# A convolution and an attention in one kernel: the block factors move to the copy of the seeds, and the first unit's maxima are taken 1024 pairs at a time

## The chip, the core and the metric

The kernel runs on one core of a Trainium2 chip. The metric is the time of the whole program on the device in microseconds (us). A core has a matrix engine (PE, with its weight loads shown as PEld), a vector engine (DVE), a scalar engine (ACT), a general engine (POOL) and a queue that issues transfers (SP). Each takes its instructions in program order and waits for the others by semaphores. Matrix results land in PSUM, eight banks of 128 x 512 float32; everything else lies in SBUF.

## What is computed

Two results are put side by side, each 2048 x 448. One is a long convolution of `u` with a kernel `K` made from complex powers, the other a full attention with 16 heads of 28 channels.

```python
# A: u [2048, 448]
P = exp((A * dt)[:, :, None] * pos)          # A complex, [448, 256]
K = 2.0 * einsum("dn,dnl->dl", C, P).real    # [448, 2048]
a = irfft(rfft(u_t, 4096) * rfft(K, 4096))[:, :2048].T + u * D_skip
# B: x [2048, 448]
q, k, v = split_heads(x @ wqkv)              # 16 heads of 28
p = softmax(q @ k.T * 28 ** -0.5)
b = concat_heads(p @ v) @ wo
return concatenate([a, b], -1)
```

## The kernel before

**First stage** (lines 213 to 536). The projections of `x` are made and written to DRAM as high and low halves, and seeds of the powers are made for each of the 56 blocks of 8 channels and written to DRAM too (`sd_d`). Four pools hold PSUM there: `ps_w` (three buffers `pm`), `ps_t` (two buffers `pt`), `ps_n`, `ps_x` (lines 219 to 222). At its end (lines 528 to 535) the maxima of the first unit are taken. A unit is 512 queries of a group of 4 heads; there are 16. The softmax subtracts a query's maximum over all 2048 keys, which is put as two rows into the query tile `qhat`, so that the score product already holds it. For each head and each 128 queries (`i`, 16 of them) `max_mm` makes four products: `kc` 0 is the query times the difference of two key halves (`kdif`), of which ACT takes the positive part (`rl`); `kc` 1 is the query times the second half, and DVE adds `rl` and takes the maximum, so that one operation covers 512 pairs of keys; `kc` 2 and 3 are plain products over 512 keys each, which DVE reduces. `max_join` takes the maximum of the three partial results, `max_end` turns it and `max_put` writes it into `qhat` by two transfers. `more` (line 528) deals the products out to the five buffers `pt` and `pm`. A scheduler may move instructions in this first stage.

**The loop** (lines 1007 to 1070) has 256 steps, 16 for each unit, and from line 856 on every instruction stays in program order. Each step walks through `ORDER` (line 34): `m0 s0 m1 s1 v f pv f v k m2 s2 m3 s3 w v`. `s` is a score product of 128 keys and its exponential on ACT, `pv` the products of the previous step with the values. `m0` to `m3` are the four products of `max_mm` for the unit after next. `f` is a slot for one background task, taken from queues (`slot`, line 950): the three products of a block of the convolution kernel (`m_due`: `part0` twice and `part1`), the transform of `u` (`u_due`), output projections (`p_due`), and, late in the loop, `spectrum` tasks and then `finish` tasks (`f_slot`). `v` takes one operation from the queue `powers["g"]` for DVE. `k` may begin a block and issues up to three operations from `powers["e"]` for POOL.

**A block** of the convolution kernel: `load_sd` brings its seeds `sdb`; `k_seeds` (line 605) copies the seeds of `e` at its first call and those of `g` at its second, one call at `k` of a step; `k_factors` (line 615) makes `fz` from three parts of `sdb` by three DVE operations of 128 x 96, both operands of each in SBUF; `k_start` (line 622) copies a part of `fz` to PSUM (`zg`) on ACT; `e_power` (line 626) issues nine POOL operations that build `e` from its seeds and `fz`; `g_powers` (line 640) gives nine DVE operations that build `g`, each with one operand in PSUM. `k_begin` (line 976) starts block `b` when `K0 + b * KP <= s` (`KP` is 3.5 steps) **and** both queues `powers` are empty. It fills them: nine operations of `g_powers`, then `k_factors` of the next block as a tenth entry (lines 982 and 983), and nine of `e_power`. The block's products fall due 4, 5 and 6 steps later (`KD`, line 990).

**Hand-over** (line 1015): when no block is left, the PSUM banks of `ps_g` and `ps_m` become one pool of four (`ps_f`), which the second half of the `spectrum` tasks needs. `spectrum` (line 768) multiplies with `u`'s transform on DVE (`pr`) and combines on POOL (`p`, 64 x 448, four a job); `finish` (line 811) loads `ut`, scales it on POOL and adds it on DVE (`ot`). A `finish` job is loaded three steps ahead (`FL`). What is left after the last step runs in the loop at line 1074.

Of the kernel before, what the change touches and what calls it, by code (L numbers as in the profile page):

```python
# [8 lines left out]
F32 = mybir.dt.float32  # L9
F32R = mybir.dt.float32r  # L10
I32 = mybir.dt.int32
AF = mybir.ActivationFunctionType
ALU = mybir.AluOpType
AX = mybir.AxisListType
PSUM = bass.MemoryType.PSUM
# [8 lines left out]
HG = H // G  # L24
CQ = 512
NQ = L // CQ
# [24 lines left out]
NB = D // 8  # L51
# [40 lines left out]
def body(ctx, tc, a, out):  # L92
    nc = Engines(tc)
# [4 lines left out]
    def pool(stack, name, bufs=1, space=None, side=None):  # L98
        kw = {} if space is None else {"space": space}
        if side:  # L100
            kw["side"] = side
        return stack.enter_context(tc.tile_pool(name=name, bufs=bufs, reuse_waits="tile", **kw))
# [21 lines left out]
    ps_w, n_ring = [None, 3], [0]  # L124
# [6 lines left out]
    q_p = pool(att, "q_p", side="right")  # L131
# [12 lines left out]
    kt_g, kd_g, q_u, m_u, mh_u, o_u, rl_u = {}, {}, {}, {}, {}, {}, {}  # L144
# [29 lines left out]
    def max_mm(u, i, kc, ps=w_tile):  # L174

        if i == 0 and kc == 0:
            m_u[u] = q_p.tile([128, HG, 4, 3], F32, name="mx", bufs=2)
        j, t = divmod(i, 4)
        pm = ps()
        q, kt = q_u[u][:, j, t * 128:(t + 1) * 128], kt_g[u // NQ][j]  # L180
        mx = m_u[u][:, j, t, max(kc - 1, 0):max(kc - 1, 0) + 1]
        if kc == 0:
            nc.tensor.matmul(pm, q, kd_g[u // NQ, j], start=True, stop=True)
            rl_u[u, i] = kd_p.tile([128, CQ], F32, name="rl", bufs=2)
            nc.scalar.activation(rl_u[u, i], pm, AF.Relu)
        elif kc == 1:
            kb = kt.rearrange("p (c s n) -> p c s n", c=NQ, s=2)[:, :2, 1, :]
            nc.tensor.matmul(pm.rearrange("p (c n) -> p c n", c=2), q, kb, start=True, stop=True)
            rl = rl_u.pop((u, i))
            nc.vector.tensor_tensor_reduce(rl, pm, rl, 1.0, -3.0e38, ALU.add, ALU.max, mx)  # L190
        else:
            nc.tensor.matmul(pm, q, kt[:, kc * CQ:(kc + 1) * CQ], start=True, stop=True)
            nc.vector.tensor_reduce(mx, pm, axis=AX.X, op=ALU.max)

    def max_join(u):
        m_u[u, 1] = q_p.tile([128, HG * 4], F32, name="m1", bufs=2)
        nc.vector.tensor_reduce(m_u[u, 1], m_u[u].rearrange("p a b c -> p (a b) c"), axis=AX.X, op=ALU.max)

    def max_end(u, ps):
        nc.tensor.transpose(ps[:16, :128], m_u[u, 1], ident)  # L200
        mh = q_p.tile([16, 2, 128], F32R, name="mh")
        nc.vector.tensor_scalar(mh[:, 0, :], ps[:16, :128], -1.0, None, op0=ALU.mult)
        nc.vector.scalar_tensor_tensor(mh[:, 1, :], ps[:16, :128], -1.0, mh[:, 0, :].bitcast(F32),
                                       op0=ALU.mult, op1=ALU.subtract)
        mh_u[u] = mh

    def max_put(u):
        for i in range(2):
            nc.sync.dma_start(q_u[u][DH + i:DH + i + 1, :, :].rearrange("p h (t q) -> p (h t) q", t=4).bitcast(F32),
                                mh_u[u][:, i, :].bitcast(F32))  # L210


    with ExitStack() as st:
        sst, xst, wst = ExitStack(), ExitStack(), ExitStack()
        t_p = pool(sst, "t_p")
        s_p = pool(sst, "s_p")
        x_p = pool(xst, "x_p")
        y_p = pool(wst, "y_p", side="right")
        ps_w[0] = pool(st, "ps_w", 1, PSUM)
        ps_t = pool(st, "ps_t", 2, PSUM)  # L220
        ps_n = pool(st, "ps_n", 2, PSUM)
        ps_x = pool(st, "ps_x", 1, PSUM)

        xns = {}

# [35 lines left out]
        t = a["A_log_dt"]  # L261
# [263 lines left out]
                for c in range(NQ):  # L525
                    load_v(0, c)
        xst.close()
        more = [lambda: ps_t.tile([128, CQ], F32, name="pt")] * 2 + [w_tile] * 3
        for i in range(16):
            for kc in range(4):  # L530
                max_mm(0, i, kc, more[(4 * i + kc) % 5])
        nc.scalar.activation(half_pi[:1], half_pi[:1], AF.Exp)
        max_join(0)
        max_end(0, ps_t.tile([128, CQ], F32, name="pt"))
        max_put(0)
        sst.close()


# [66 lines left out]
    def k_seeds(b):  # L605

        if b not in es:
            es[b] = e = g_p.tile([128, 2, 16, N2], F32, name="e", bufs=2)
            nc.scalar.activation(e[:, :, :, :8], sds[b][:, :F_G].rearrange("p (c h e) -> p c h e", c=2, e=8), AF.Copy)
        else:  # L610
            g = g_p.tile([128, 2, 16, N1], F32, name="g", bufs=2)
            nc.scalar.activation(g[:, :, :, :4], sds[b][:, F_G:F_Z].rearrange("p (c h e) -> p c h e", c=2, e=4), AF.Copy)
            egs[b] = es.pop(b), g

    def k_factors(b):
        fzs[b] = fz = g_p.tile([128, 3, 6 * 16], F32, name="fz", bufs=2)
        mg, cs, sn = (sds[b][:, F_Z + 96 * i:F_Z + 96 * i + 96] for i in range(3))
        nc.vector.tensor_tensor(fz[:, 0], mg, cs, ALU.mult)
        nc.vector.tensor_tensor(fz[:, 2], mg, sn, ALU.mult)
        nc.vector.scalar_tensor_tensor(fz[:, 1], mg, -1.0, sn, op0=ALU.mult, op1=ALU.mult)  # L620

    def k_start(b):
        zgs[b] = ps_g.tile([128, CQ], F32, name="zg")
        nc.scalar.activation(zgs[b][:, :Z_G].rearrange("p (f n) -> p f n", f=3), fzs[b][:, :, 48:], AF.Copy)

    def e_power(b, i, q):

        t, m = egs[b][0], 8 << i
        zz = fzs[b].rearrange("p f (k h) -> p k f h", k=6)
        if q == 0:  # L630
            zr = zz[:, i, 0, :][:, None, :, None].to_broadcast([128, 2, 16, m])
            nc.gpsimd.tensor_tensor(t[:, :, :, m:2 * m], t[:, :, :, :m], zr, ALU.mult)
        elif q == 1:
            uts[0] = g_p.tile([128, 2, 16, 32], F32, name="eu")[:, :, :, :m]
            zi = zz[:, i, 1:3, :][:, :, :, None].to_broadcast([128, 2, 16, m])
            nc.gpsimd.tensor_tensor(uts[0], t[:, ::-1, :, :m], zi, ALU.mult)
        else:
            nc.gpsimd.tensor_tensor(t[:, :, :, m:2 * m], t[:, :, :, m:2 * m], uts[0], ALU.add)

    def g_powers(b):  # L640

        t, zg = egs[b][1], zgs[b]
        zz = zg[:, :Z_G].rearrange("p (f k h) -> p k f h", k=3, f=3)
        tt = nc.vector.tensor_tensor

        def first(i, m):
            tt(t[:, :, :, m:2 * m], t[:, :, :, :m], zz[:, i, 0, :][:, None, :, None].to_broadcast([128, 2, 16, m]), ALU.mult)

        def second(i, m, c):
            n = c.stop - c.start  # L650
            u = zg[:, CQ // 2:CQ // 2 + n * 16 * m].rearrange("p (c h m) -> p c h m", c=n, m=m)
            zi = zz[:, i, 1 + c.start:1 + c.stop, :][:, :, :, None].to_broadcast([128, n, 16, m])
            tt(u, t[:, ::-1, :, :m][:, c], zi, ALU.mult)
            return lambda: tt(t[:, c, :, m:2 * m], t[:, c, :, m:2 * m], u, ALU.add)
        both, u = slice(0, 2), {}

        def lowest():
            first(0, 4)
            second(0, 4, both)()
        ops = [lowest, lambda: first(1, 8), lambda: u.update(a=second(1, 8, both)), lambda: u["a"](), lambda: first(2, 16)]  # L660
        for c in (slice(0, 1), slice(1, 2)):
            ops += [lambda c=c: u.update(a=second(2, 16, c)), lambda: u["a"]()]
        return ops
# [196 lines left out]
        max_mm(1, 0, kc)  # L860
    for _ in range(2):
        k_seeds(0)
    k_factors(0)

    urgent, back = collections.deque(), collections.deque()
    powers = {"g": collections.deque(), "e": collections.deque()}
# [109 lines left out]
    def k_begin(s_):  # L976
        if not (k_due and K0 + k_due[0] * KP <= s_ and k_due[0] in egs and not powers["e"] and not powers["g"]):
            return
        b = k_due.popleft()
        k_start(b)  # L980
        powers["g"] += g_powers(b)
        if b + 1 < NB:
            powers["g"].append(lambda: k_factors(b + 1))
        powers["e"] += [lambda i=i, q=q: e_power(b, i, q) for i in range(3) for q in range(3)]
        p0, p1, p2 = k_mm(b)

        def m1():
            p1()
            done["mm"] = b
        m_due.extend((s_ + KD + i, t_) for i, t_ in enumerate((p0, m1, p2)))  # L990
        last[0] = b
# [15 lines left out]
    for s in range(NS):  # L1007
        u, kt = divmod(s, NK)
        sm = s + NK + min(LEAD, 1 + s // 2)
        more = s in (2, 4)  # L1010
# [62 lines left out]
    s = NS  # L1073
# [65 lines left out]
```

## Time and profile before

| what | value |
|---|---|
| median of three runs | 1309.37 us (1307.53 to 1311.9) |
| the profiled execution | 1310.93 us |
| its span in the profile | 1308.8 us |
| granted PE clock, mean | 0.98 |
| the last two score products start | from 1274.75 us of the span on |

The profile gives times from the start of the span. A row of a timeline has the start, the time taken, the engine, and output<-input by the program's names; "x2" merges two neighbours, and a bracket gives the idle time before and what ended it. A row of a group has busy time and the mean of one in ns. Every program line that issues an instruction goes through one helper, so all rows bear its line L76, and one goes by names. The rows that the argument needs stand in the prediction.

### The profile page before, as it was taken

The page shows a single profiled execution, that of the slowest core. Times are in us where ns is not written, and L with a number is a line of the kernel's source. Part 1 is how long each engine was busy: PE and PEld are TensorE (multiplying, and loading weights), DVE is VectorE, ACT ScalarE, POOL GpSimd, SP SyncE. Part 2 cuts the span into 40 slices and gives each one's busy share as a digit, 9 for nine tenths or more (in the row PEclk, how much of TensorE's full clock was granted, in tenths as well). Part 3 has the DMA queues.
Part 4 walks back from the last instruction along what each step waited for, and adds up shares of the span by engine and source line. Part 5 has one row for each costly group of instructions (what it writes and reads, how often), then busy time and mean ns, then how long its engine had stood idle before and what let it go on. Part 6 is the DMA issues. An engine that isn't in the chain of part 4 may idle for free.

```text
span 1308.8 us, 32327 instructions
## 1 busy us (share of the span) xinstructions
PE 1225.8 (94%) x12177; PEld 686.0 (52%) x12177; DVE 948.6 (72%) x2194; ACT 963.7 (74%) x2048; POOL 839.0 (64%) x656
## 2 busy tenths in 40 slices
PE   6888976899999999999999999999999999999996
PEld 5666853455555555555555555555555555454332
DVE  5676678878877887777788888888888958453221
ACT  4878873588888888888878888888877657565451
POOL 2455641467777787777788888878879849235341
PEclk9989988899999999999999999999999999999998
DMA  6777779546864545487524225431454533269577
GB/s 195 230 255 267 260 235 294 157 93 153 183 151 105 126 147 167 112 215 196 155 71 95 74 51 136 109 96 39 109 151 124 171 99 107 82 187 287 170 228 192
DMA packets 200084, 205.30 MB, mean 157 GB/s; under 512 B 95992, under 2 KB 158520, under 8 KB 197880
## 3 DMA queue, kind: packets, MB, share of 16 engines
q1 hardware_dynamic: 199928, 203.24, 55.3%
q8 instruction: 96, 1.57, 0.5%
q14 instruction: 60, 0.49, 0.1%
HBM read 120.74 MB, written 82.18 MB: 155 GB/s over the span
## 4 chain that ended last, share of the span: by engine, by line
PE 71%; DVE 8%; DMA 4%; POOL 4%; ACT 3%; issue 2%; SPq 1%; POOLq 0%; DVEq 0%; ACTq 0%
PE pm L76 40%; PE pss L76 16%; PE po L76 16%; DVE mx L76 2%; DMA ut<-in_A_u 2%; POOL p L76 1%; DVE rl L76 1%; ACT tri L76 1%; DVE tri L76 1%; POOL e L76 1%; SPq L76 1%; DVE pr L76 1%; DVE mh L76 1%; ACT sg L76 1%; DVE fz L76 1%
## 5 line engine op out<-in xcount | busy, mean ns | idle before, releaser
L76 ACT ACTIVATE p<-pss 128x512 f32<-128x512 f32 x1024 | 561.9, 610 | 127.9 <-PE pss L76 125.7
L76 DVE TENSOR_REDUCE mx<-pm 128x1 f32<-128x512 f32 x500 | 321.7, 684 | 128.7 <-PE pm L76 127.6
L76 PE MATMUL pss<-qhat,khat 128*128 128x512 f32 x1024 | 403.0, 400 | 0.7 <-ACT p L76 0.6
L76 PE MATMUL pm<-khat,qhat 128*128 128x512 f32 x749 | 330.3, 443 | 9.6 <-DVE mx L76 6.8
L76 POOL TENSOR_TENSOR e<-e,fz 128x256 f32<-128x256 f32 x168 | 203.2, 1209 | 202.3 <-PE pss L76 84.0
L76 PE MATMUL po<-p,v 128*32 128x512 f32 x2048 | 269.8, 594 | 0.0
L76 PEld LDWEIGHTS pm<-khat,qhat 128*128 128x128 f32 x749 | 141.5, 189 | 220.1 <-DVE mx L76 41.5
L76 POOL TENSOR_TENSOR e<-e,eu 128x256 f32<-128x256 f32 x168 | 247.9, 1475 | 13.2
L76 PEld LDWEIGHTS pss<-qhat,khat 128*128 128x128 f32 x1024 | 190.5, 189 | 40.3 <-issue 9.6
L76 POOL TENSOR_TENSOR eu<-e,fz 128x256 f32<-128x256 f32 x168 | 201.7, 1200 | 0.0
L76 DVE CUSTOM_DVE_ANT_0 rl<-pm,rl 128x512 f32<-128x512 f32 x249 | 170.8, 686 | 31.6 <-ACT rl L76 27.3
L76 ACT ACTIVATE rl<-pm 128x512 f32<-128x512 f32 x249 | 151.0, 606 | 19.3 <-PE pm L76 18.9
L76 DVE TENSOR_TENSOR g<-g,zg 128x128 f32<-128x128 f32 x392 | 162.1, 413 | 3.6
L76 POOL TENSOR_TENSOR p<-pr,pr 64x448 f32<-64x448 f32 x64 | 73.3, 1146 | 96.9 <-PE pm L76 61.7
L76 PE MATMUL pm<-xh,khat 112*128 112x512 f32 x256 | 89.0, 430 | 20.6 <-DVE kb L76 7.8
L76 PE MATMUL pm<-kdif,qhat 128*128 128x512 f32 x249 | 102.2, 410 | 4.4 <-DVE pr L76 2.2
L76 DVE TENSOR_TENSOR zg<-g,zg 128x128 f32<-128x128 f32 x224 | 87.7, 392 | 4.7
L76 PEld LDWEIGHTS pm<-e,g 128*32 128x32 f32 x3584 | 58.2, 109 | 45.6 <-issue 23.5
L76 DVE TENSOR_TENSOR pr<-pm,ub 128x448 f32<-128x448 f32 x64 | 36.9, 619 | 53.5 <-PE pm L76 38.7
L76 ACT ACTIVATE y<-pm 128x448 f32<-128x448 f32 x48 | 26.3, 547 | 66.9 <-PE pm L76 44.7
L76 PE MATMUL pm<-e,g 128*32 128x64 f32 x3584 | 73.1, 221 | 1.9 <-POOL e L76 1.9
L76 PEld LDWEIGHTS po<-p,v 128*32 128x32 f32 x2048 | 55.1, 110 | 31.8 <-issue 27.7
(129 smaller groups left out, 1435.6 us busy)
## 6 DMA issues: line engine op xcount, KB each, us to landing
sdb<-sd SPq DMA_DIRECT2D x56, 336.0 KB
khat<-k SPq DMA_DIRECT2D x64, 256.0 KB
qhat<-q SPq DMA_DIRECT2D x64, 256.0 KB
sd<-sg SPq DMA_DIRECT2D x8, 1456.0 KB
k<-hl SPq DMA_DIRECT2D x16, 512.0 KB
q<-hl SPq DMA_DIRECT2D x16, 512.0 KB
v<-v SPq DMA_DIRECT2D x32, 256.0 KB
mw<-in_mw SPq DMA_DIRECT2D x16, 512.0 KB
```

Of the source, the lines that this page charges most:

```text
L76: i = f(*args, **kw)
```

## The change

Two edits.

1. `k_factors(b)` is called at the end of the second call of `k_seeds(b)`, right after the copy of `g`'s seeds. The tenth entry of `powers["g"]` and the call ahead of the loop go.
2. The first unit's maxima are written out anew. The four PSUM pools of the first stage are closed ahead of them and a pool of four double banks (`ps_2`) is opened. The queries of each head are negated once on POOL (`nq`). For each `i` one double bank `pd` takes the two difference products (the second as `q` times the third key quarter plus `nq` times the fourth, added up in PSUM), another, `pb`, the two products of the second members: five products in place of four. One ACT operation takes the positive part of 1024 elements, one DVE operation adds and takes the maximum over 1024 pairs. Its result goes straight to the joined tile, so `max_join` goes. The later units keep `max_mm`.

```diff
-        more = [lambda: ps_t.tile([128, CQ], F32, name="pt")] * 2 + [w_tile] * 3
+        psx.close()
+        m_p = pool(mst, "m_p")
+        ps_2 = pool(psm, "ps_2", 4, PSUM)
+        nq = m_p.tile([128, HG, CQ], F32R, name="nq")
+        m_u[0, 1] = q_p.tile([128, HG * 4], F32, name="m1", bufs=2)
         for i in range(16):
-            for kc in range(4):
-                max_mm(0, i, kc, more[(4 * i + kc) % 5])
+            j, t = divmod(i, 4)
+            ts = slice(t * 128, (t + 1) * 128)
+            q, kt = q_u[0][:, j, ts], kt_g[0][j]
+            if t == 0:
+                nc.gpsimd.tensor_scalar(nq[:, j], q_u[0][:, j].bitcast(F32), -1.0, None, op0=ALU.mult)
+            pd, pb = (ps_2.tile([128, 2, CQ], F32, name="p2") for _ in range(2))
+            kb = kt.rearrange("p (c s n) -> p c s n", c=NQ, s=2)[:, :2, 1, :]
+            mm = nc.tensor.matmul
+            mm(pd[:, 0], q, kd_g[0, j], start=True, stop=True)
+            mm(pd[:, 1], q, kt[:, 2 * CQ:3 * CQ], start=True, stop=False)
+            mm(pd[:, 1], nq[:, j, ts], kt[:, 3 * CQ:], start=False, stop=True)
+            mm(pb[:, 0].rearrange("p (c n) -> p c n", c=2), q, kb, start=True, stop=True)
+            mm(pb[:, 1], q, kt[:, 3 * CQ:], start=True, stop=True)
+            rl = m_p.tile([128, 2, CQ], F32, name="rl2", bufs=2)
+            nc.scalar.activation(rl, pd, AF.Relu)
+            nc.vector.tensor_tensor_reduce(rl, pb, rl, 1.0, -3.0e38, ALU.add, ALU.max, m_u[0, 1][:, i:i + 1])
         nc.scalar.activation(half_pi[:1], half_pi[:1], AF.Exp)
-        max_join(0)
-        max_end(0, ps_t.tile([128, CQ], F32, name="pt"))
+        max_end(0, ps_2.tile([128, 2, CQ], F32, name="p2")[:, 0])
         max_put(0)
...
             egs[b] = es.pop(b), g
+            k_factors(b)
...
-    k_factors(0)
...
         powers["g"] += g_powers(b)
-        if b + 1 < NB:
-            powers["g"].append(lambda: k_factors(b + 1))
```

More of the change, by code (lines that the diff above doesn't have):

```diff
@@ L213, in body @@
     with ExitStack() as st:
-        sst, xst, wst = ExitStack(), ExitStack(), ExitStack()
+        sst, xst, wst, mst, psx, psm = (ExitStack() for _ in range(6))
         t_p = pool(sst, "t_p")
@@ L218, in body @@
         y_p = pool(wst, "y_p", side="right")
[L219 to L222, printed above, removed]
+        ps_w[0] = pool(psx, "ps_w", 1, PSUM)
+        ps_t = pool(psx, "ps_t", 2, PSUM)
+        ps_n = pool(psx, "ps_n", 2, PSUM)
+        ps_x = pool(psx, "ps_x", 1, PSUM)
         xns = {}
@@ L527, in body @@
         xst.close()
-        more = [lambda: ps_t.tile([128, CQ], F32, name="pt")] * 2 + [w_tile] * 3
-        for i in range(16):
-            for kc in range(4):
-                max_mm(0, i, kc, more[(4 * i + kc) % 5])
+        psx.close()
[3 more added lines that the diff above has]
+        m_u[0, 1] = q_p.tile([128, HG * 4], F32, name="m1", bufs=2)
+        for i in range(16):
+            j, t = divmod(i, 4)
[14 more added lines that the diff above has]
+            nc.vector.tensor_tensor_reduce(rl, pb, rl, 1.0, -3.0e38, ALU.add, ALU.max, m_u[0, 1][:, i:i + 1])
         nc.scalar.activation(half_pi[:1], half_pi[:1], AF.Exp)
-        max_join(0)
-        max_end(0, ps_t.tile([128, CQ], F32, name="pt"))
+        max_end(0, ps_2.tile([128, 2, CQ], F32, name="p2")[:, 0])
         max_put(0)
+        psm.close()
+        mst.close()
         sst.close()
```

## Prediction

> **What bounds the kernel now.** I read the page first (span, engines), then the busy time of stretches, then timelines of single steps, then the waits and the chain of work that ended last.
>
> ```profile
> span 1308.8 us, 32327 instructions
> PE 1225.8 (94%) x12177; PEld 686.0 (52%) x12177; DVE 948.6 (72%) x2194; ACT 963.7 (74%) x2048; POOL 839.0 (64%) x656
> ```
> ```profile
> 738.90:963.20 224.30, 223.51 (x2454) 123.70 (x2452) 197.37 (x501) 189.66 (x425) 184.61 (x144) 1.00 0.37 87
> 963.20:1035.00 71.80, 68.18 (x839) 38.10 (x837) 62.68 (x142) 51.62 (x114) 60.33 (x49) 1.00 0.54 171
> 1193.60:1277.50 83.90, 77.81 (x848) 31.59 (x844) 18.75 (x39) 43.95 (x83) 32.90 (x27) 1.00 0.68 214
> 1277.50:1308.80 31.30, 18.94 (x261) 7.96 (x260) 5.15 (x14) 3.40 (x6) 6.28 (x3) 0.86 0.70 187
> ```
> The columns are the stretch, its length, and busy us of PE, PEld, DVE, ACT, POOL, then the clock. The first row is four units (64 steps, 16 blocks): PE has 0.8 us of idle in 224.3, so the loop's middle is PE's, with DVE at 88% and POOL at 82% close behind. In the later rows PE has holes: 3.6, 6.1 and, after the last step, 12.4 us.
>
> **The change part by part.** *The pace of the blocks.* Before, `g`'s queue has ten entries and takes three a step; stepping through the loop's conditions, the tenth is taken after `k` of the third step, so a block begins every 4 steps, the last at step 220, with the hand-over at 227. With nine entries the queue is empty at `k` of the third step: gaps of 3 and 4 alternate, the last block begins at 193, the hand-over is at 200. The same products are made earlier; in a stretch that is PE's alone this costs nothing.
>
> *Where the factors land.* They move from the last `v` of a step to its `k`, one step ahead of the block's begin: between the two `v` operations and the reduction of `m2`.
>
> ```profile
> 830.16 0.39 PE L76 MATMUL pm<-kdif,qhat 128*128 128x512 f32 x1
> ...
> 833.62 0.39 PE L76 MATMUL pm<-kdif,qhat 128*128 128x512 f32 x1
> ...
> 834.08 0.39 PE L76 MATMUL pm<-khat,qhat 128*128 128x512 f32 x1
> ...
> 836.67 0.39 PE L76 MATMUL pm<-kdif,qhat 128*128 128x512 f32 x1
> ```
> ```profile
> 833.22 1.28 DVE L76 TENSOR_REDUCE mx<-pm 128x1 f32<-128x512 f32 x2
> ...
> 836.43 1.28 DVE L76 TENSOR_REDUCE mx<-pm 128x1 f32<-128x512 f32 x2
> 837.63 0.42 DVE L76 TENSOR_TENSOR fz<-sdb 128x96 f32<-128x96 f32 x2
> 837.97 0.25 DVE L76 SCALAR_TENSOR_TENSOR fz<-sdb 128x96 f32<-128x96 f32 x1
> ```
> `kdif` opens a step: 3.46 us with a block's product in its slot (830.16 to 833.62), 3.05 without. `m2` and `m3` reduce from 3.06 us into the heaviest step, 2.81 in the next. Freeing `m2`'s buffer at 833.86 (half of the 1.28) is what the next `m1` at 834.08 needs: three `pm` buffers leave about 0.1 us. Three factor operations (0.5 us) ahead of it thus reach PE nearly whole, about 0.4 us a block where a step has one task; where it has two, `m2` itself comes some 0.5 us later and nothing is lost. The present place costs some too: in four steps (823.96 to 837.63, below) the sum is 3 x 3.46 + 3.05 = 13.43, the row 13.67, so 0.2.
>
> *Who runs beside them.*
>
> ```profile
> 823.96 0.42 DVE L76 TENSOR_TENSOR fz<-sdb 128x96 f32<-128x96 f32 x2
> ```
> ```profile
> 824.38 0.66 POOL L76 TENSOR_TENSOR e<-e,fz 128x256 f32<-128x256 f32 x1 [1.77 <-ACT rl L76]
> ...
> 833.94 2.39 POOL L76 TENSOR_TENSOR e<-e,eu 128x1024 f32<-128x1024 f32 x1
> ```
> ```profile
> 653.45 2.33 POOL L76 TENSOR_TENSOR e<-e,eu 128x1024 f32<-128x1024 f32 x1
> ```
> ```profile
> 653.67 2.40 DVE L76 TENSOR_TENSOR fz<-sdb 128x96 f32<-128x96 f32 x2
> ```
> ```profile
> 979.39 4.86 POOL L76 TENSOR_TENSOR p<-pr,pr 64x448 f32<-64x448 f32 x4 [3.12 <-PE pm L76]
> ```
> ```profile
> 980.70 1.34 DVE L76 TENSOR_TENSOR fz<-sdb 128x96 f32<-128x96 f32 x2
> 981.97 1.20 DVE L76 SCALAR_TENSOR_TENSOR fz<-sdb 128x96 f32<-128x96 f32 x1
> ```
> Normally the factors run while POOL rests (1.77 us), and POOL's nine operations follow; they end at 836.33, 12.37 us after the factors began. In the two other places the factors met a running POOL operation, and ended just behind it: 2.40 us in place of 0.42 (653.67), 1.34 and 1.20 (980.70). So I take it that they wait for the POOL operation under way. [...] After the change POOL's own wait is gone, and what is late is DVE: the next factors are wanted after 3 steps, 3 x 3.46 + 0.25 (3.06 less 2.81) + 0.36 (the stall of the gap before) = 11.0 us, and POOL needs 12.37. The wait is 1.35 us, in POOL's ninth operation; behind it on DVE stands `m2`'s reduction and behind that PE's `m1`. After a 4-step gap (13.5 us and more) POOL is done.
>
> Price of a pair of blocks with one task a step: 1.35 + 0.35 (what the displaced operations cost beside it) = 1.7 for the 3-step gap, 0.36 for the other, less 0.4 for the present place: 1.66. Going through the slots, 13 pairs lie behind step 104: 21.6 us, less 3.5 because seven of their short gaps hold a unit's end work in a slot and last 0.45 to 0.75 us longer (estimates from the row sums): 18. Before step 104 the transform of `u` adds a task to about two steps in three; of 14 three-step gaps 11 are shorter than 12.37 by 0.2 to 1.9 us, 8 us together, of which two-task steps absorb all but some 3. **Sum +21.** Bounds: 0 if DVE's wait stays inside the buffers' slack; 29.4 (the unshortened waits, 8.1 and 21.3) + 13 x 0.9 = 41 if nothing absorbs any.
>
> *The end of the loop.* From 963.2 on, 6 factor calls met POOL's `p` as at 980.70.
>
> ```profile
> 981.80 1.37 DVE fz L76 x2
> ...
> 1000.09 1.37 DVE fz L76 x2
> ```
> ```profile
> 1137.13 0.94 PE L76 MATMUL pm<-p,mw 128*32 128x224 f32 x16
> 1138.00 0.50 PE L76 MATMUL pm<-khat,qhat 128*128 128x512 f32 x1
> ```
> The first two rows are of the chain that ended last, so this wait holds up the end; between them lie four steps, 18.3 us. A spectrum task costs PE 0.87 (1137.13 to 1138.00); 13.43 and four of these are 16.9. So 1.4 us is lost each time, -8.4, since the blocks are through at step 193 and the spectra start at 194. The steps with three slots (from 237 on) hold 14 spectrum tasks in place of 26; PE's 6.1 us of holes there over 26 tasks make 12 x 0.23: -2.8. Against it, the last block's POOL work now has a `p` join (4.86 us, 979.39) in front of its last three operations: +5, once. Four finish tasks more run inside the loop, at most 0.87 each: +3.5. **Sum -3** (-12 to +5).
>
> *After the last step.*
>
> ```profile
> 1293.76 6.72 DMA ut<-in_A_u
> ```
> ```profile
> 1295.28 1.15 DVE L76 TENSOR_TENSOR ot<-pm,ut 128x224 f32<-128x224 f32 x3 [2.94 <-PE pm L76]
> 1302.74 1.28 DVE L76 TENSOR_TENSOR ot<-pm,ut 128x224 f32<-128x224 f32 x4 [6.32 <-POOL ut L76]
> ```
> Here 12 finish tasks are left; after the change 8, one job less: the job whose `ut` lands at 1300.5 and whose sums start at 1302.74, 7.5 us behind the group before. Some 2 more come where `ut` no longer holds DVE ahead of the last unit's scaling. **-10** (-12 to -6).
>
> *The first unit's maxima.*
>
> ```profile
> L76 DVE TENSOR_REDUCE mx<-pm 128x1 f32<-128x512 f32 x20 | 13.1, 683 | 0.0
> L76 DVE TENSOR_REDUCE mx<-pt 128x1 f32<-128x512 f32 x12 | 7.9, 683 | 0.0
> L76 DVE CUSTOM_DVE_ANT_0 rl<-pm,rl 128x512 f32<-128x512 f32 x9 | 6.1, 683 | 1.3 <-PE pm L76 1.3
> L76 DVE CUSTOM_DVE_ANT_0 rl<-pt,rl 128x512 f32<-128x512 f32 x7 | 4.8, 682 | 2.5 <-ACT rl L76 2.5
> ```
> ```profile
> 183.83 1.90 DVE L76 TENSOR_TENSOR tri<-tri 128x1680 f32<-128x1680 f32 x1
> ```
> ```profile
> 219.41 3.74 SPq L76 DMA_DIRECT2D v<-v  x4
> ...
> 236.41 1.27 SPq L76 DMA_DIRECT2D qhat<-mh  x2
> ```
> ```profile
> 203.00:207.40 4.40, 3.97 (x9) 2.94 (x10) 2.54 (x7) 1.19 (x2) 0.00 (x0) 0.50 0.96 270
> 207.40:222.00 14.60, 12.68 (x34) 5.63 (x32) 14.28 (x31) 4.92 (x9) 0.00 (x0) 0.99 1.05 318
> ...
> 227.00:235.50 8.50, 6.26 (x15) 3.18 (x15) 7.53 (x18) 1.79 (x3) 0.00 (x0) 0.76 0.96 335
> 235.50:239.00 3.50, 3.21 (x6) 1.49 (x6) 2.24 (x7) 0.60 (x1) 0.00 (x0) 0.50 0.13 29
> ```
> DVE bounds this stage: 31.9 us of 32. One operation over 1024 lies between one over 512 (0.68) and two (1.37); by the slope to 1680 elements (1.90) it is 1.2, which I take: 16 x 1.3 with its read-out = 21. Five products at the row pitch of 0.23 (833.62 to 833.85) are 1.15, so PE stays under DVE; ACT's 1024 is at most two of its 0.6. The four negations lie on an idle POOL; the first delays the first unit by at most one POOL operation of that size (1.06). But the gain of 11 isn't all had. SP issues a transfer when an earlier one has landed: by the `v` rows the last key quarter lands towards 222.8, four of the 16 maxima wait for it, and the end comes near 230. Then `mh` queues behind transfers that keep the queues 96% busy to 235.5 (fourth window row). It lands near 237 where it did at 239. **-2** (-4 to +2).
>
> The granted clock is 0.50 in the first 4.4 us and again from 235.5. [...]
>
> **Sum:** -2 + 21 - 3 - 10 = +6. 1310.93 + 6 = 1316.9 for an execution like the profiled one, which is 1.6 above the median of the runs: **1315**.
>
> **The rivals.** *Faster:* the factors' wait doesn't reach PE. For it: POOL rests 1.77 us a block now, and the 653.67 case coincides with a PE wait for POOL's `e`, so PE's loss isn't proven there. Against it: 0.1 us of slack and the 1.4 us a block behind 963. With 6 us left of 21, which the displaced operations cost by themselves: 1300. It decides wherever three steps last longer than 12.4 us. *Cancelled:* the waits reach PE for some 13 us: 1307. *Slower still:* PE at half clock in the maxima. It would take 16 x 5 x 0.42 (twice the pitch) = 34 us from 203.4, past 235.3: +5 in place of -2, 1322. The trace has 0.99 from 207.4 on, so it is unlikely. [...] *Both factor reads wait:* as at 980.70 in each of 55 blocks, 55 x 1.4 = 77 in place of 21: 1371; POOL's next operation there was ready, whereas `e`'s next waits for the factors, so I hardly expect it. *The change doesn't do what it says* (blocks stay at 4 steps): the order of the built instructions speaks against it.
>
> **How the numbers follow.** A difference of 0.3%, 4 us, is about what a measurement of this kernel tells from none. Forecast (slower, 1313.5 to 1336) 0.42; half clock 0.05; both reads 0.02: slower 0.49. Cancelled 0.18. Faster 0.33. The range runs from the faster rival with the other terms at their low bounds, halfway (1291), to the forecast with all waits unabsorbed (1336); the likeliest case's own is 1313.5 to 1336.
>
> **What would show it.** Blocks begin every 3 and 4 steps, the last power of `g` near the unit 12 boundary; `fz` takes over 1 us at every second block from step 104 on and ends with POOL's operation, with `m1` on PE late behind it; a unit there takes over 58 us, not 56; no `fz` meets `p`; one `ut` load less behind the last step; the first score product near 237. If `fz` stays at 0.25 us, or PE stays gapless beside long ones, the forecast is wrong on the fast side; if the wait is there but the end gives back over 20 us, too.

## The result, and the profile after

The changed kernel takes **1316.09 us** (median, 1314.95 to 1316.53) against 1309.37; the ratio is 1.0048, 95% interval 1.0033 to 1.0063. It is slower by half a per cent, and the forecast was 1315. The profiled execution is the 1316.09 one, its span 1314.3.

The page of the changed kernel, first two lines:

```profile
span 1314.3 us, 32353 instructions
PE 1222.8 (93%) x12193; PEld 691.5 (53%) x12193; DVE 944.9 (72%) x2161; ACT 973.1 (74%) x2048; POOL 845.3 (64%) x660
```

PE does no more than before (1225.8 there); the loss is idle time. The next two fences show where. Both are the busy time of the same three stretches: units 0 to 11 from the first score product, units 12 to 15 up to the last score product, and the rest. Columns as in the prediction: the stretch, its length, busy us of PE, PEld, DVE, ACT, POOL, then the clock, the transfers' share and GB/s. First the kernel before:

```profile
239.01:963.20 724.19, 718.33 (x7753) 389.23 (x7753) 601.28 (x1506) 602.67 (x1366) 555.34 (x434) 1.00 0.49 122
963.20:1275.08 311.88, 297.93 (x3382) 148.16 (x3381) 181.30 (x395) 196.70 (x402) 175.94 (x141) 1.00 0.53 165
1275.08:1308.80 33.72, 21.36 (x270) 8.38 (x268) 5.26 (x15) 4.49 (x8) 6.28 (x3) 0.87 0.73 197
```

and the changed kernel:

```profile
234.89:991.32 756.43, 731.85 (x8296) 398.60 (x8297) 646.03 (x1601) 616.50 (x1406) 635.67 (x497) 1.00 0.49 119
991.32:1290.08 298.76, 286.72 (x2870) 141.76 (x2869) 144.09 (x304) 185.22 (x362) 98.02 (x81) 0.99 0.57 175
1290.08:1314.30 24.22, 18.77 (x238) 7.24 (x236) 3.97 (x10) 4.49 (x8) 4.17 (x2) 0.97 0.50 133
```

Read length and PE's busy time together. Units 0 to 11 are 32.2 us longer, but 13.5 us of that is work (731.85 less 718.33): products of the blocks that were made in units 12 to 15 before. The other 18.7 is PE standing still: 24.6 us of holes where there were 5.9 (23.9 and 23.8 in two later profiles with the same units 0 to 11, `after_again` and `e9_last_block`). Units 12 to 15 are 13.1 shorter. PE has 11.2 less work there: 13.5 of the blocks' products are gone, and 2.3 of finish products came in from behind the last step. Its holes fall by only 1.9. The end is 9.5 shorter, and the loop starts 4.1 earlier. Sum: -4.1 + 32.2 - 13.1 - 9.5 = +5.5, the difference of the spans.

What the holes wait for, from the view of PE's waits over units 7 to 11 of the changed kernel (total, times, longest):

```profile
PE pm L76 <- DVE mx L76: 16.3, 16, 1.4
```

and over the same units of the kernel before:

```profile
PE pm L76 <- DVE mx L76: 1.0, 5, 0.2
```

One such hole, from a timeline of the changed kernel:

```profile
845.41 2.39 POOL L76 TENSOR_TENSOR e<-e,eu 128x1024 f32<-128x1024 f32 x1
...
846.62 1.47 DVE L76 TENSOR_TENSOR fz<-sdb 128x96 f32<-128x96 f32 x2
...
848.01 0.24 DVE L76 SCALAR_TENSOR_TENSOR fz<-sdb 128x96 f32<-128x96 f32 x1
...
848.18 1.27 DVE L76 TENSOR_REDUCE mx<-pm 128x1 f32<-128x512 f32 x2
...
848.91 0.50 PE L76 MATMUL pm<-khat,qhat 128*128 128x512 f32 x1 [1.25 <-DVE mx L76]
```

POOL's ninth operation runs from 845.41 to 847.80. The first factor starts at 846.62, takes 1.30 us and is done 0.1 behind POOL's end; a pair that takes 0.42 takes 1.47. Behind it the reductions of `m2` and `m3` are late, and behind them PE. In units 7 to 11 every second block shows it: the trace has a hole of 0.7 to 1.45 us in PE behind the factors of each of the eleven three-step gaps, and none above 0.1 right behind ten of the eleven four-step gaps.

At the end of the first stage, groups of the changed kernel between 196 and 234 us:

```profile
L76 DVE CUSTOM_DVE_ANT_0 rl<-p,rl 128x1024 f32<-128x1024 f32 x16 | 19.5, 1224 | 8.1 <-ACT rl L76 7.7
...
L76 ACT ACTIVATE rl<-p 128x1024 f32<-128x1024 f32 x16 | 16.3, 1027 | 10.9 <-PE p L76 10.9
```

and its stretches from the first product of the maxima on:

```profile
201.40:210.80 9.40, 8.71 (x20) 6.41 (x21) 3.61 (x6) 3.25 (x4) 5.82 (x4) 0.51 1.04 355
210.80:228.10 17.30, 15.54 (x62) 10.18 (x60) 16.02 (x26) 13.08 (x13) 0.00 (x0) 1.00 1.03 280
228.10:234.90 6.80, 2.15 (x7) 0.95 (x7) 2.46 (x6) 0.60 (x1) 0.00 (x0) 0.72 1.01 362
```

1024 pairs take DVE 1.22 us where two operations over 512 took 1.37, and two further reductions over 512 are gone, so `mh` is issued at 228.76 instead of 236.41. But in the last row PE is idle for 4.6 of 6.8 us while the transfers run at a full share: the first score product waits for `mh`, 16 KB in two transfers that were issued 5.8 us behind `sd<-sg` of 1456 KB; from their issue to the product it is 6.1 us, and it is 2.6 in the kernel before, where the transfers' share is 0.13 in the row of 235.50. Timelines of the changed kernel's SP and PE:

```profile
222.93 0.37 SPq L76 DMA_DIRECT2D sd<-sg  x1
228.76 1.27 SPq L76 DMA_DIRECT2D qhat<-mh  x2
```
```profile
234.89 0.80 PE L76 MATMUL pss<-qhat,khat 128*128 128x512 f32 x1 [4.19 <-DMA qhat<-mh]
```

### The profile page after: what moved, and what is told of

It reads as the page before. It is cut to its first block, busy times and chain, and to the rows that moved or that the text cites. A ratio compares the mean times of both kernels' runs of the same rounds, so it can differ in the third digit from the quotient of the medians.

```text
span 1314.3 us, 32353 instructions
## 1 busy us (share of the span) xinstructions
PE 1222.8 (93%) x12193; PEld 691.5 (53%) x12193; DVE 944.9 (72%) x2161; ACT 973.1 (74%) x2048; POOL 845.3 (64%) x660
## 4 chain that ended last, share of the span: by engine, by line
PE 73%; DVE 9%; ACT 4%; DMA 2%; POOL 2%; issue 2%; SPq 0%; ACTq 0%; POOLq 0%; DVEq 0%
PE pm L76 40%; PE pss L76 15%; PE po L76 15%; DVE fz L76 2%; DVE mx L76 2%; PE p L76 2%; DVE rl L76 1%; ACT p L76 1%; DVE tri L76 1%; POOL p L76 1%; ACT rl L76 1%; ACT tri L76 1%; DVE g L76 1%; POOL qhat L76 1%; DMA qhat<-q 1%
## 5 line engine op out<-in xcount | busy, mean ns | idle before, releaser
L76 DVE TENSOR_REDUCE mx<-pm 128x1 f32<-128x512 f32 x480 | 308.2, 683 | 113.6 <-PE pm L76 112.4
L76 PE MATMUL pm<-khat,qhat 128*128 128x512 f32 x720 | 315.5, 439 | 22.8 <-DVE mx L76 21.7
L76 POOL TENSOR_TENSOR e<-e,eu 128x256 f32<-128x256 f32 x168 | 248.1, 1477 | 13.2
L76 PEld LDWEIGHTS pm<-khat,qhat 128*128 128x128 f32 x720 | 135.2, 188 | 229.1 <-DVE mx L76 59.5
L76 PEld LDWEIGHTS pss<-qhat,khat 128*128 128x128 f32 x1024 | 191.1, 189 | 49.0 <-issue 10.8
L76 DVE CUSTOM_DVE_ANT_0 rl<-pm,rl 128x512 f32<-128x512 f32 x240 | 165.1, 688 | 49.8 <-ACT rl L76 48.0
L76 ACT ACTIVATE rl<-pm 128x512 f32<-128x512 f32 x240 | 145.4, 606 | 5.0 <-PE pm L76 4.8
L76 PE MATMUL pm<-kdif,qhat 128*128 128x512 f32 x240 | 96.5, 402 | 1.3 <-DVE mx L76 0.8
L76 ACT ACTIVATE ub<-pm 128x224 f32<-128x224 f32 (+1 forms) x96 | 38.5, 446 | 42.2 <-PE pm L76 41.8
```

The costliest lines, as they stand in the source:

```text
L76: i = f(*args, **kw)
```

## The experiments

### Each edit alone

`e1_factors` is the kernel before with the first edit only, `e2_maxima` with the second only; each is the other half of the diff undone. All ratios from here on are against runs of the kernel before that were taken beside the experiment.

> The first edit alone: the factors at the copy of g's seeds, the first unit's maxima as before. If the two edits add up, with the loop starting 4.1 us earlier owed to the maxima, this is after plus 4.1: 10.8 over before, 1320 us. Rival: the maxima's head start is lost again in the loop, because the loop then meets transfers that are still under way; then this is as after, 1316.

> The second edit alone: the maxima in pairs, the factors in g's queue as before, a block every four steps. If the edits add up: 4 us under before, 1305 us, first score product at 235. Rival: no difference, 1309.

Measured: 1321.37 us (ratio 1.0088, 1.0074 to 1.0102) and 1310.21 (1.0006, 0.9997 to 1.0015), both against 1309.99. So the first edit costs 11.4 us, close to the 10.8 expected. The second alone gives nothing that can be measured, against the expectation; in its profile the first score product starts at 238.2, not 235, though `mh` is issued at 231.46. The changed kernel's start at 234.9 was thus not simply the edit's. The last experiment returns to this.

### The place of the factors, at the old pace

```diff
-K0, KP, KD, UP = 0, 3.5, 4, 3
+K0, KP, KD, UP = 0, 4, 4, 3
```

> The changed kernel with KP at 4 in place of 3.5: the factors stay ahead of m2's reduction, but a block begins every four steps, the last at step 220, so POOL is done when the next factors come. Theory: no fz meets POOL's e, the place alone costs nothing that can be measured against its old place, and the end is that of before with p met six times: 1305 us (1303 to 1308). Rival (the place ahead of m2's reduction costs 0.4 us in each of 55 blocks): 1327.

Measured: 1342.46 us (1.0251, 1.0236 to 1.0265), 26 slower than the changed kernel. The theory was wrong by 37 us, and the rival by 15. Two stretches of this kernel, units 8 to 11 and unit 13:

```profile
747.70:980.00 232.30, 225.28 (x2453) 123.73 (x2453) 198.91 (x502) 192.62 (x425) 184.86 (x144) 1.00 0.36 84
...
1059.00:1147.30 88.30, 79.86 (x918) 42.23 (x917) 60.87 (x136) 53.65 (x115) 59.57 (x48) 0.96 0.33 98
```

Units 8 to 11 took 224.3 before: the place alone costs 8.0 us for 16 blocks, 0.5 a block, and no factor operation there lasts longer than 0.26. The trace has a hole of about 0.4 us in PE behind every set of factors there. Ahead of `m2`'s reduction, 0.5 us of DVE reach PE nearly whole at this pace. Units 12 and 13 took 71.8 and 81.5 before and take 79.0 and 88.3 here, because the factors meet `p`; timelines of this kernel's POOL, then of its DVE:

```profile
996.98 4.84 POOL L76 TENSOR_TENSOR p<-pr,pr 64x448 f32<-64x448 f32 x4 [5.09 <-PE pss L76]
```
```profile
997.09 1.32 DVE L76 TENSOR_TENSOR fz<-sdb 128x96 f32<-128x96 f32 x2
998.33 1.18 DVE L76 SCALAR_TENSOR_TENSOR fz<-sdb 128x96 f32<-128x96 f32 x1
999.43 1.28 DVE L76 TENSOR_REDUCE mx<-pm 128x1 f32<-128x512 f32 x2
```

Two factors wait as the prediction had it at the old place, and here with `m2`'s reduction behind them.

### No second operand in SBUF

```diff
+            if b:
+                nc.scalar.activation(zgs[b - 1][:, Z_G:Z_G + 96], sds[b][:, F_Z:F_Z + 96], AF.Copy)
...
+        if b:
+            mg = zgs[b - 1][:, Z_G:Z_G + 96]
```

> The changed kernel, but one operand of the factors is first copied to PSUM by ACT (one more ACT operation a block), so that no factor operation has two operands in SBUF. Pace, place and number of DVE operations stay. Theory (the factors wait for the POOL operation under way because both have to read SBUF): every fz takes about 0.25 to 0.35 us, PE's 12.3 us of idle in the four units from 750.8 on fall to about 3, and the loop gives back some 17 us: 1299 us (1295 to 1303). Rival (the three operations cost by standing ahead of m2's reduction, whatever their operands): 1316. Rival (the pace itself, POOL's nine operations in three steps, holds PE): 1316 as well, with PE waiting for POOL's e.

Measured: 1318.43 us (1.0059, 1.0045 to 1.0073). The time is that of the two rivals, but the trace shows that it is not for their reason. Groups of this kernel, and a factor pair beside a running POOL operation:

```profile
L76 DVE TENSOR_TENSOR fz<-zg,sdb 128x96 f32<-128x96 f32 x110 | 23.0, 251 | 2.5
L76 DVE SCALAR_TENSOR_TENSOR fz<-zg,sdb 128x96 f32<-128x96 f32 x55 | 13.6, 248 | 0.0
```
```profile
849.05 2.40 POOL L76 TENSOR_TENSOR e<-e,eu 128x1024 f32<-128x1024 f32 x1
...
850.60 0.42 DVE L76 TENSOR_TENSOR fz<-zg,sdb 128x96 f32<-128x96 f32 x2
```

With one operand in PSUM none of 165 operations waits, POOL or not: they take 251 and 248 ns on average, the medians of the kernel before are 249 and 250, and the pair beside POOL's 2.40 us takes 0.42. So the run shows that the wait ends with an operand in PSUM; that reading SBUF is its reason stays the author's theory. But the added copy stands in ACT's queue ahead of the exponentials, and the view of ACT's waits over units 7 to 11 has a row that the changed kernel has not:

```profile
ACT zg L76 <- ACT ko L76: 13.9, 19, 0.9
```

The name in that row misleads: 21 of the 23 copies there start 0.08 us behind the end of a DVE operation `zg<-g,zg` on the same PSUM tile, while `ko` had ended long before, so ACT waits for DVE. PE's waits for `mx` there fall from 16.3 to 7.3 us, yet the five units take 298.0 us in place of 301.3. One wait was in part exchanged for another, so this experiment could not say what the wait is worth. The next ones could.

### Shorter POOL work, and a later place

As reference the changed kernel ran again beside the next experiments.

> The changed kernel once more, beside the next three on the same chip, as their reference: 1316 us. If the first score product comes at 235 again, the head start of 4.1 us belongs to the second edit; if it comes between 236.5 and 238.5, as in the three other kernels with the same maxima, it was that one execution's.

Measured: 1316.69 us (1.0058, 1.0044 to 1.0072). Its first score product comes at 238.8, so the start of the same kernel differs by 3.9 us between two executions. `sd<-sg` was already issued 3.5 later (226.44).

```diff
-        powers["e"] += [lambda i=i, q=q: e_power(b, i, q) for i in range(3) for q in range(3)]
+        powers["e"] += [lambda i=i, q=q: e_power(b, i, q) for i in range(3) for q in range(3) if i + q < 4]
```

> The changed kernel without POOL's last addition of each block (the upper half of e lacks a term, so the convolution is not the reference's). POOL's nine operations become eight and end 2.4 us earlier, before the next factors come; what DVE, ACT and PE do stays. Theory of the prediction (the wait for POOL is most of the loop's loss): 13 waits of 1.35 us and some 3 us of the u phase go, and step 197 shortens by 2.4: 1296 us (1292 to 1300). Rival (the place ahead of m2's reduction is most of it, as the kernel with four steps a block says with 0.5 us a block): the waits go but PE is held as long by the displaced operations: 1309 (1306 to 1312).

Measured: 1298.0 us (0.9918, 0.9903 to 0.9933), 18.7 under its reference. The theory's value; the rival falls. The two profiled executions differ by 17.8: 12.6 in units 0 to 11, 4.5 in units 12 to 15 (the theory had 2.4 there) and 0.7 in the start. Units 0 to 11 of this kernel:

```profile
238.10:980.86 742.76, 731.86 (x8296) 399.10 (x8297) 633.00 (x1601) 614.79 (x1406) 504.69 (x442) 0.99 0.49 121
```

Against the changed kernel's 756.43: PE and ACT do the same, the stretch is 13.7 us shorter (12.6 against the reference's 755.3), and DVE's busy time falls by 13.0 although it executes the same instructions. That is the wait, which counts as busy time. PE still has 10.9 us of holes, 5.0 more than before. Its waits over units 7 to 11 (16.3 in the changed kernel):

```profile
PE pm L76 <- DVE mx L76: 3.9, 14, 0.7
```

The next kernel puts the factors later:

```diff
-            k_factors(b)
+            f_due.append(b)
...
+        if f_due:
+            k_factors(f_due.pop())
```

(The second part stands at the end of a step, behind the last `v`.)

> The changed kernel with the factors called at the last v of the step in which the seeds of g are copied, behind the reductions of m2 and m3, where the kernel before has them; pace and POOL's work stay, so factors still meet POOL in the gaps of three steps. Rival (the place is most of the loss, 0.5 us in each of 55 blocks): 1290 us (1286 to 1296). Theory of the prediction (the wait is most of it, and DVE's queue behind it holds PE wherever it stands): 1312 (1309 to 1316).

Measured: 1313.52 us (1.0032, 1.0021 to 1.0044), 3.2 under the reference and the theory's value. Beside the wait the place is worth only that; the wait stays, and what is behind it now is the next step's work (timeline of this kernel):

```profile
845.85 1.78 DVE L76 TENSOR_TENSOR fz<-sdb 128x96 f32<-128x96 f32 x2
...
848.46 0.50 PE L76 MATMUL pm<-kdif,qhat 128*128 128x512 f32 x1 [0.51 <-DVE mx L76]
...
849.86 0.50 PE L76 MATMUL pm<-khat,qhat 128*128 128x512 f32 x1 [0.67 <-DVE mx L76]
```

### The wait removed with all work done

If the loss is that POOL is not through after three steps, it is enough to even out the distances. In this kernel the factors of a block with a three-step gap stand at the last `v`, the others at `k`:

```diff
+            if b in egs:
+                if s_ + 1 - begun[0] > 3:
+                    k_factors(b)
+                else:
+                    f_due.append(b)
```

> The changed kernel, in which the factors of a block that begins three steps after the last stand at the last v of the step, and those of one that begins four steps after stay at k. So POOL gets about 12.2 us from one set of factors to the next in both gaps instead of 10.5 and 14. Number of operations and pace stay. Theory (the loss in the three-step gaps is the wait for POOL's ninth operation): most of the 12.5 us that the kernel without that operation gained in the loop comes back with all work done: 1304 us (1301 to 1308). Rival (that gain was owed to less POOL work as such, contention at large): 1313 to 1316.

Measured: 1304.19 us (0.9962, 0.9950 to 0.9974). Units 0 to 11 of this kernel:

```profile
234.90:979.23 744.33, 734.60 (x8297) 400.46 (x8297) 632.58 (x1601) 614.93 (x1406) 634.24 (x497) 0.99 0.49 121
```

12.1 us less than the changed kernel (11.0 less than its second profile) with the same POOL work (634.24 against 635.67), and DVE is 13.4 us less busy. In units 7 to 11 the sets of factors begin 12.1 to 13.2 us apart, and PE's waits there are down to:

```profile
PE pm L76 <- DVE mx L76: 1.5, 5, 0.7
```

The rival (less POOL work as such) falls. That half of the factors stand later is not the reason either: with all of them there, in `e6_late_factors`, the gain was 3.2.

### The last block's POOL work

In the changed kernel, timelines of POOL and of PE in unit 12:

```profile
1008.82 4.78 POOL L76 TENSOR_TENSOR p<-pr,pr 64x448 f32<-64x448 f32 x4 [8.89 <-DVE pr L76]
1013.67 1.91 POOL L76 TENSOR_TENSOR e<-e,fz 128x1024 f32<-128x1024 f32 x1
```
```profile
1019.90 1.08 PE L76 MATMUL pm<-e,g 128*32 128x64 f32 x32 [6.45 <-POOL e L76]
```

POOL rests 8.9 us before the joins with ready operations of `e` behind them; PE then waits 6.45 us.

```diff
-                for _ in range(3):
+                for _ in range(3 if k_due else 9):
```

> The changed kernel with all nine POOL operations of the last block issued when it begins, so that none stands behind the first joins p. In the changed kernel POOL rests 8.9 us in front of those joins, waiting for DVE's pr, with three ready operations of e behind them, and PE then waits 6.4 us for e. Theory: that wait goes and nothing takes its place: 1310 us (1308 to 1312). Rival: the joins now end later and PE waits for p instead: 1313 to 1316.

Measured: 1307.69 us (0.9988, 0.9974 to 1.0001), just under the theory's range. Unit 12 of this kernel takes 66.1 us in place of 74.1, and POOL's timeline there is now:

```profile
1002.84 2.38 POOL L76 TENSOR_TENSOR e<-e,eu 128x1024 f32<-128x1024 f32 x1
1007.79 4.81 POOL L76 TENSOR_TENSOR p<-pr,pr 64x448 f32<-64x448 f32 x4 [2.58 <-DVE pr L76]
```

### The factors on POOL

A block every four steps, and:

```diff
-        nc.vector.tensor_tensor(fz[:, 0], mg, cs, ALU.mult)
-        nc.vector.tensor_tensor(fz[:, 2], mg, sn, ALU.mult)
-        nc.vector.scalar_tensor_tensor(fz[:, 1], mg, -1.0, sn, op0=ALU.mult, op1=ALU.mult)
+        nc.gpsimd.tensor_tensor(fz[:, 0], mg, cs, ALU.mult)
+        nc.gpsimd.tensor_tensor(fz[:, 2], mg, sn, ALU.mult)
+        nc.gpsimd.tensor_scalar(fz[:, 1], fz[:, 2], -1.0, None, op0=ALU.mult)
```

> The changed kernel with a block every four steps and the three factor operations on POOL in place of DVE (the third as the negated second). DVE has nothing ahead of m2's reduction and POOL's order takes the place of every wait, with p too. If place and wait of DVE's factors are all that the edit costs: the loop is that of before less 0.2 us a block and less the six waits for p of 1.4 us: 1290 to 1298 us. Rival: POOL is late with the factors near p and holds ACT's copy zg in front of the exponentials: 1310 or more.

Measured: 1318.91 us (1.0074, 1.0056 to 1.0092). The rival came: units 7 to 11 are as before (280.4 us), so DVE's 0.5 us a block at the old place had cost PE nothing there, but in units 12 and 13 the factors stand behind `p` in POOL's queue, and the wait goes on to ACT and PE (views of their waits in units 12 and 13):

```profile
ACT zg L76 <- POOL fz L76: 15.2, 6, 3.7
```
```profile
PE pss L76 <- ACT p L76: 10.8, 6, 2.2
```

### Three mends together

The kernels with two places and with the last block's POOL work in one, and `load_wo` eight slots later. In the changed kernel its POOL memset waited 7.9 us for a tile, with a block's operations behind it, and the next factors met POOL's operations one after the other (timelines of POOL and DVE):

```profile
652.96 0.85 POOL L76 MEMSET ua<- 128x896 f32 x1 [7.89 <-PE pm L76]
```
```profile
660.41 2.92 DVE L76 TENSOR_TENSOR fz<-sdb 128x96 f32<-128x96 f32 x2
```

```diff
-            load_wo()
+            soon_slot(8, load_wo)
```

> Both mends of the two kernels before in one, and the load of wo's tiles (a POOL memset that waits 7.9 us for its tile, with a block's operations behind it) eight slots later. If the three places are independent: 1316.7 less 12.5, less 6.4, less some 3.5: 1294 us (1290 to 1299), under both kernels. Rival: the three-step pace leaves too little for POOL anyway, 1303 or more.

Measured: **1291.77 us** (0.9866, 0.9854 to 0.9879), faster than the changed kernel by about 24 and than the kernel before by 17.8. Its first two stretches:

```profile
236.20:976.02 739.82, 731.91 (x8297) 399.39 (x8297) 630.42 (x1601) 614.79 (x1406) 633.79 (x497) 1.00 0.50 122
976.02:1266.84 290.82, 285.18 (x2871) 141.20 (x2869) 144.14 (x304) 185.08 (x362) 100.36 (x81) 1.00 0.58 180
```

PE has 7.9 us of holes in units 0 to 11 (24.6 in the changed kernel) and 5.6 in units 12 to 15 (12.0).

### The maxima, once more

The kernel with the three mends, and the old maxima:

> The kernel with the three mends, but with the first unit's maxima as before, to settle what the second edit is worth: alone it gave nothing (1310.21 against 1309.99 us), on top of the first edit 5. In the eleven profiles so far with the new maxima mh's transfer is issued 6 us earlier on average than in the two with the old, the first score product starts 1.7 us earlier, and the loop's fourth step 2.9. If the second edit is worth that start: 1294 us (1293 to 1295.5). Rivals: nothing, 1291.8; 5 us, 1297.

Measured: 1296.43 us (0.9898, 0.9878 to 0.9918), by the ratios 4.2 us more than with the new. That is above the expected range and nearer the 5 us rival. The traces show two parts. The loop's fourth step starts at 251.3 here and at 248.9 with the new maxima. And the last step of unit 14 takes 8.2 us here and in `e1_factors`, but 6.3 in every kernel with both edits at the pace of 3.5. The traces put this on a transfer `ut`; POOL's timeline with the old maxima (this kernel), then with the new (the kernel before):

```profile
1191.16 2.10 POOL L76 TENSOR_TENSOR ut<-ut,dsk 128x896 f32<-128x896 f32 x1 [8.80 <-DMA ut<-in_A_u]
```
```profile
1187.83 2.12 POOL L76 TENSOR_TENSOR ut<-ut,dsk 128x896 f32<-128x896 f32 x1 [7.35 <-DMA ut<-in_A_u]
```

It was issued at 1181.56 and 1179.92, so it took 9.6 and 7.9 us, and in the first case POOL's scaling stands in front of the joins `p` that PE waits for. Why the same transfer takes 1.7 us longer there stays open. Why the second edit alone showed nothing is answered in part: at the pace of four steps that last step of unit 14 takes 4.0 us with the old maxima (the kernel before) and with the new (`e2_maxima`), so this part cannot show there. The start in its profile was a late one (238.2), but its interval reaches down to a gain of 0.4 us only, and the rest stays open.

## Why the prediction was right, point by point

*The pace* was as stepped through (the last factors come in step 192, for a block that begins at 193), with products of 13.5 us moved from units 12 to 15 to those before, at no cost in themselves.

*Where the factors land, +21: measured +18.7* (18.0 in the two later profiles). The mechanism is shown by two different interventions, less POOL work and evened-out distances, which take back 13.7 and 12.1 us. The sizes are off a little: the waits are 13.7 where the prediction's own parts made 17 (13 times 1.35, less 3.5, plus 3). The rest is 5.0, where the displacement made 4; 2 of it is a step that nobody priced, `load_wo`'s memset (7.6 us for the step in place of 5.6).

That the displacement came out near 4 is in part luck, because two of its terms were wrong and cancel. A block behind a four-step gap costs PE next to nothing (0.36 in the prediction). And the old place cost nothing (0.2 a block in the prediction, 0.4 a pair): PE has no hole in the four steps from 823.96 on, and the first of them, which takes 3.7 us where the prediction's sum has 3.46, takes 3.7 us as well in the kernel in which POOL makes the factors. Nor is the price of a four-step gap a rule: at a steady pace of four steps the new place costs 0.5 us a block. There the factors stand in the step without a block's product (3.04 us), behind the four-step gaps of the changed kernel in steps of 3.5 us and more; that this is the reason was not tested.

*Both reads wait* came about where `p` runs (the kernel with four steps a block), as in the row of 980.70 before, and once in the changed kernel beside operations of `e`: at 660.41 two factors took 1.04 and 1.96 us.

*The end of the loop, -3: measured +0.4* (-13.1 for units 12 to 15, with 13.5 of work moved away). The mis-sized term that an experiment shows is the last block's `e` behind a join: +5 in the prediction, which took the join's own 4.86. What PE pays is 8.0, since the joins also wait for DVE's `pr` while `e` is ready behind them. With 8 in place of 5 the sum is 0. The other terms were not measured one by one; the finish tasks brought 2.3 us of PE's work in where the prediction had 3.5.

*After the last step, -10: measured -9.5.* One load of `ut` less, as forecast.

*The maxima, -2: -4.1 in the profiled execution, -0.2 in the second.* DVE's price was right (1.22, forecast 1.2), and so was what takes it back, `mh` behind the queued transfers. In all eleven profiles with the new maxima the first score product starts 11.5 to 12.5 us after the issue of `sd<-sg`, and a later `mh` (4.6 to 5.8 us behind that issue) does not make it later. In the three with the old maxima it is 12.9 to 13.9. Measured so, the edit is worth 1.2 us at the start. When `sd<-sg` is issued varies from 222.1 to 227.0 us, on average alike in both groups, so about 2 of the 4.1 us are this execution's luck. The last key quarter was not what ended the stage: the transfers behind it were.

*The rivals.* "Faster" falls: PE is not gapless beside long factors. "Half clock" happened in part (0.51 granted for the first 9.4 us of the maxima, 1.00 then); what sets the clock no run here shows. It should have cost nothing, since the transfers end the stage (PE idle for 4.6 of the last 6.8 us). The gains of the end nearly cancel the loss in the loop, as the cancelled case had it, but the loss is the larger by 5.5. (By the prediction's own terms the top of its range is 1335, not 1336.)

## What to carry to other kernels

Before an in-order operation is moved earlier, lay its new time beside the engine that the traces show it waiting for (POOL here): what counts is not its own duration (0.25 us) but what it may have to wait out (about 1.1 us on average here, 16.3 over the 15 sets of factors that waited in the changed kernel) and which queue stands behind it. When the distance between two users of a slow engine alternates between too short and too long, move one of the two by half a step rather than the pace. And a queue in which ready work stands behind work that is not ready (`e` behind `p`, 8 us) is mended by the order of issue alone.

## What the runs showed that was not expected

- A factor's wait for POOL's operation stands inside the DVE instruction (1.30 us at 846.62) and counts as busy: DVE's busy time fell by 13.0 and 13.4 us when the waits went, with the same 1601 instructions. A DVE share that rises without new work was the sign of it here.
- Two `mh` transfers of 8 KB took 6.1 us from issue to the product that needs them (228.76 to 234.89) with the transfers at a full share (up to 7.8 in the other profiles with the new maxima), and 2.6 us in the kernel before (236.41 to 239.01).
- POOL's tensor-tensor over 128 x 96 takes 0.39 us and its product with a constant 0.45, where DVE takes 0.25; its negation of 128 x 512 takes 1.49, longer than a tensor-tensor of `e` of that size (1.06).
